# Two heads side by side in TensorE's rows, in scores and second GEMM, and another order of transposes between two batches

## The chip, the cores and the metric

The kernel runs on one core of one Trainium2 chip. The core has five engines with a queue each: TensorE (PE, matrix products into PSUM), VectorE (DVE), ScalarE (ACT), GpSimd (POOL) and SyncE (SP), which here only issues transfers (DMAs). An instruction starts when it has reached the head of its engine's queue and the semaphores that it waits for are set. The metric is the device time of one execution in microseconds (us).

## The reference

Eight batches of eight heads of causal attention over 576 tokens with 64 channels a head, with a forgetting factor that enters as a decay, then a dense layer pair with an exact GELU between:

```
scores = (q @ k^T) / 8 + (cum[s] - cum[t]), cum = cumsum(log(clip(f, 1e-4, 1)))
attn   = softmax(causal(scores));  x = attn @ v          # x as 4608 tokens x 512
out    = gelu(x @ w_in) @ w_out                          # 512 -> 2048 -> 512
```

Inputs and the output are float32; the kernel computes its products in bfloat16 with float32 sums.

## The kernel before

**Stages.** Each batch b has two stages. In its attention stage the four pairs of heads i = 0..3 go through scores, exp, and the product with v. In its first GEMM the 512 channels of x meet `w_in` in 16 blocks of 128 hidden channels, each four matmuls of 128x512, and GELU moves each block to SBUF as `g`. The second GEMM of batch b-1 is not a stage of its own: its 64 matmuls ("fill") are dealt out among the attention instructions of batch b by a table. 64 tokens of each batch (512 to 575, the "tail") don't fill a block of 128; they are collected in `tails` and go through both GEMMs at the end as a ninth block.

**Scores.** A pair's scores are held transposed, keys in partitions, in four PSUM tiles `s` with two banks each, one bank a head (tables `STILES`, with 448, 448, 448 and 320 columns a head). `kT[i]` holds the keys of both heads of pair i, one in partitions 0 to 63, one in 64 to 127. `qA[i]` and `qB[i]` hold one head's queries each in their half of the partitions and zeros in the other, so a matmul over all 128 partitions gives one head's scores (line 308). ACT takes exp of a whole tile (line 323), POOL sets what lies above the diagonal to zero (line 325); in batch 0 and the first pair of batch 1 PE adds a large negative number there instead (line 317). `s` tiles come from a pool of two, so scores of tile k wait until the exp of tile k-2 is done.

**Product with v.** `attend` (line 344) runs 15 small matmuls of 65 columns a head: v was multiplied by the decay weights on POOL (`weigh_v`, line 292), and its 65th column gives the softmax sum. `normalize` (lines 359 to 370) divides on DVE, into `x` and the tail `xt`. `x` has to be transposed for the first GEMM: SP issues a transposing DMA a pair (`x_dma`, line 386) and one for the tail (line 392). In batch 0 PE does it instead (`to_xT`, line 380).

**Queries and keys.** POOL's queue loads q and k of batch b+2 while batch b is worked on (line 102). Before the scores they are transposed: in batch 0 by PE (`transposes_first`), in batch 1 by PE (`transposes_pe`), from batch 2 on by transposing DMAs on SP (`transpose_dma`, line 262, four a batch: q and k, heads 0 to 3 and 4 to 7). DVE then sorts them into `qA`, `qB` and `kT` during the first GEMM of the batch before (`untangle`, line 276, eight copies a pair).

**What sets the order.** The program is scheduled by hand: each engine's instructions stand in the order in which the code emits them. `FILL[i][t]` says how many fill matmuls follow tile t of pair i, and its last row how many stand before, between and after the two heads of the last pair. `take(fill, n)` emits n of them; the generator `gemm2` opens a PSUM tile `ps` for every 128 tokens, sums over 16 blocks of hidden channels, and lets DVE copy the sum to SBUF (line 451) and SP store it (line 458).

Of the kernel before, what the change touches and what calls it, by code (L numbers as in the profile page):

```python
# [14 lines left out]
P = 128  # L15
# [35 lines left out]
def kernel(  # L51
# [96 lines left out]
    def zero_halves(pairs):  # L148
        for i in pairs:
            nc.vector.memset(qA[i][D:P, :], 0.0)  # L150
            nc.vector.memset(qB[i][0:D, :], 0.0)
# [23 lines left out]
    zero_halves(range(2))  # L175
# [16 lines left out]
    def transposes_first(i, which, pool, tag):  # L192

        src = qk_of[0][which]
        ps = pool.tile([P, JT, PT], BF16, tag=tag, name="ps_f")
        for h in range(2):
            for j in range(JT):
                nc.tensor.transpose(
                    ps[h * D : (h + 1) * D, j, :],
                    src[:, 2 * i + h, j * D : (j + 1) * D],  # L200
                    ident_bf[:PT, :PT],
                )

        def evac(eng, dst, r0, r1):
            op = eng.copy if eng is nc.scalar else eng.tensor_copy
            op(  # L206
                dst[r0:r1, :].rearrange("d (p j) -> d p j", j=JT),
                ps[r0:r1].rearrange("d j p -> d p j"),
            )

        if which:
            evac(nc.vector, kT[i], 0, P)
        else:
            evac(nc.vector if i else nc.scalar, qA[i], 0, D)
            evac(nc.vector, qB[i], D, P)

    def transposes_pe(b, i, pool):
# [20 lines left out]
        for which, ps in enumerate(pss):  # L238
            for h in range(2):
                dst = (qA[i], qB[i])[h] if which == 0 else kT[i]  # L240
# [26 lines left out]
    def untangle(b, i):  # L267

        for which, src in enumerate(tq_of[b]):
            for h in range(2):  # L270
                dst = (qA[i], qB[i])[h] if which == 0 else kT[i]
# [30 lines left out]
    def scores(b, i, t):  # L302
# [3 lines left out]
        for n, q0, w in STILES[t]:  # L306
            for h, qt in enumerate((qA[i], qB[i])):
                nc.tensor.matmul(  # L308
                    st[:, h, c : c + w],
                    kT[i][:, K0[n] : K0[n] + P],  # L310
                    qt[:, q0 : q0 + w],
# [65 lines left out]
    def to_xT(b, i, copy):  # L377
        ps = m_psum.tile([P, TC], BF16, tag="m", name="ps_x")
# [83 lines left out]

    def take(gen, n):
# [5 lines left out]
    def first_attention():  # L469
# [12 lines left out]
        zero_halves(range(2, HP))  # L482
# [55 lines left out]
    FILL = [[4, 6, 2, 2], [2, 2, 2, 2], [2, 2, 2, 2], [2, 2, 1, 1], [8, 0, 20]]  # L538
    FILL_1 = [[0, 4, 4, 0], [2, 2, 2, 2], [4, 4, 4, 4], [3, 3, 3, 3], [8, 0, 99]]

    def attention(b, fill, counts):
        for i in range(HP):
            for t in range(4):
# [6 lines left out]
                elif i and t == 3:  # L550
                    attend(b, i - 1, 1, (0, 1, 2, 3, 4))
                    normalize(b, i - 1, 1)
                    x_dma(b, i - 1)
                if t == 1 and i == 0 and b > 1:
                    load_v(b + 1)
                if b > 2 and t == 0 and i < 2:
                    transpose_dma(b + 1, 4 * i, 4 * i + 4)
                if b == 2 and t == 3 and i in (1, 2):
                    transpose_dma(3, 4 * i - 4, 4 * i)
                if b == 1 and (i, t) in ((0, 0), (0, 3)):  # L560
                    transposes_pe(1, 2 + t // 3, o_psum)
                if b == 1 and i == 1 and t in (0, 2):
                    weigh_v(1, 2 + t // 2)
                if b == 1 and i in (1, 2) and t == 3:
                    load_v(2, 4 * i - 4, 4 * i)
                take(fill, counts[i][t])
        i = HP - 1
        take(fill, counts[HP][0])
        attend(b, i, 0, (0, 1, 2, 3, 4))
# [4 lines left out]
        x_dma(b, i)  # L574
        x_tail_dma(b)
        if b == 1:
            transpose_dma(2, 0, 4)
            transpose_dma(2, 4, 8)
        take(fill, 999)

    for b in range(B):
        if b == 0:
            first_attention()
        else:
            attention(b, gemm2(b - 1, b == 1), FILL_1 if b == 1 else FILL)
# [3 lines left out]
        for ffb in range(n_ff):  # L589
            gemm1(b, ffb)  # L590
            if b == 0:
                if ffb in (6, 8):
                    transposes_pe(1, ffb // 2 - 3, s_psum)
# [47 lines left out]
```

## Time and profile before

| | us |
|---|---|
| median of 8 runs | 363.63 (362.56 to 364.57) |
| the profiled execution | 364.02 |
| its span, first to last instruction | 362.3 |
| PE busy in the span | 346.0 |
| ACT, DVE, POOL busy | 217.5, 179.4, 124.6 |
| time between the same points of two batches, 4 to 7 | 37.4 |

A row of the timeline gives start, length, engine, line and operation, output and inputs by name, shapes, the number of instructions that the row merges, and in square brackets how long the engine stood idle before it and what it waited for. Matmuls are pipelined: each is shown with its whole way through the array, so neighbours overlap, and the rate is read from the distance of two starts. A row of the table by stretches gives, for each engine, the busy time and in brackets the number of instructions, then the granted TensorE clock as a share of full speed, the busy share of the DMA engines, and GB/s.

### The profile page before, as it was taken

To read this page: it belongs to the slowest core of one execution; us is meant where nothing else is said; L and a number is where in the kernel's file an instruction comes from. 1 tells how busy PE (TensorE), PEld (TensorE's weight loads), DVE (VectorE), ACT (ScalarE), POOL (GpSimd) and SP (SyncE) were. 2 spreads that over 40 slices of the span, in tenths; PEclk is the share of its full clock that TensorE was granted. 3 is DMA by queue.
4 is the path that set the end of the run, shared out by engine and by line. 5 is a ranking of instruction groups with operands and counts; after the bars stand their busy time and mean duration, and the time that the engine had idled before them with its cause. 6 is when DMAs were issued, how large, how long until landed. Compare 5 with 4: busy or idle time off the path is not lost.

```text
span 362.3 us, 7046 instructions
## 1 busy us (share of the span) xinstructions
PE 346.0 (95%) x2740; PEld 188.6 (52%) x2740; DVE 179.4 (50%) x478; ACT 217.5 (60%) x298; POOL 124.6 (34%) x243
## 2 busy tenths in 40 slices
PE   7989989798998999999999999999999999999995
PEld 3764556433554456545654466446644664444443
DVE  7862884412966904592559446753676252011011
ACT  5887776255970788368845884578647973602610
POOL 7390284520447025621463055505440440000000
PEclk9999999989999999999999999999999999999999
DMA  7999999799758996397839792979520032011013
GB/s 111 169 189 191 181 171 212 173 123 198 136 125 137 191 191 123 77 179 146 160 77 168 146 188 63 150 130 207 87 81 0 34 71 80 2 58 58 2 29 87
DMA packets 106112, 44.38 MB, mean 122 GB/s; under 512 B 84896, under 2 KB 101536, under 8 KB 106080
## 3 DMA queue, kind: packets, MB, share of 16 engines
q1 hardware_dynamic: 88784, 29.78, 40.7%
q0 software_dynamic: 16896, 13.63, 25.8%
q8 instruction: 21, 0.34, 0.4%
q10 hardware_dynamic: 400, 0.52, 0.4%
q14 instruction: 11, 0.09, 0.1%
HBM read 36.85 MB, written 9.44 MB: 128 GB/s over the span
## 4 chain that ended last, share of the span: by engine, by line
PE 75%; DMA 10%; SPq 5%; DVE 4%; POOL 4%; issue 1%; POOLq 0%
PE ps L442 31%; PE ps L404 27%; PE s L308 10%; PE o L344 7%; DMA v_sb<-in_v_dram 4%; DMA tk<-k 4%; SPq L114 4%; DMA w_out_sb<-in_moe_w_out_dram 2%; DVE kT L276 1%; POOL vw L292 1%; DMA xT<-x 1%; POOL k L102 1%; DVE ot L451 1%; POOL q L102 1%; DVE qA L276 1%
## 5 line engine op out<-in xcount | busy, mean ns | idle before, releaser
L416 ACT ACTIVATE g<-ps 128x512 bf16<-128x512 f32 x144 | 86.0, 597 | 101.9 <-PE ps L404 101.8
L442 PE MATMUL ps<-w_out_sb,g 128*128 128x512 bf16 (+2 forms) x592 | 143.6, 373 | 1.3 <-DMA w_out_sb<-in_moe_w_out_dram 1.3
L404 PE MATMUL ps<-xT,w_in_sb 128*128 128x512 bf16 x512 | 115.0, 383 | 4.4 <-DMA xT<-x 3.7
L323 ACT ACTIVATE e<-s 128x896 bf16<-128x896 f32 (+1 forms) x128 | 105.3, 863 | 20.7 <-PE s L308 13.6
L325 POOL TENSOR_SCALAR_AFFINE_SELECT e<-e 128x256 bf16<-128x256 bf16 x135 | 54.2, 412 | 134.1 <-ACT e L323 132.9
L404 PEld LDWEIGHTS <-w_in_sb 128*128 128x128 bf16 x576 | 56.5, 98 | 74.9 <-issue 10.8
L451 DVE COPY ot<-ps 128x512 f32<-128x512 f32 (+2 forms) x37 | 25.1, 677 | 101.7 <-PE ps L442 101.5
L442 PEld LDWEIGHTS <-g 128*128 128x128 bf16 x592 | 52.2, 98 | 43.5 <-issue 1.5
L308 PE MATMUL s<-qA,kT 128*128 128x256 bf16 (+2 forms) x192 | 51.7, 281 | 2.6 <-DVE kT L276 1.5
L308 PEld LDWEIGHTS <-kT 128*128 128x128 bf16 x384 | 36.3, 97 | 33.8 <-issue 4.5
L292 POOL TENSOR_TENSOR vw<-v_sb,wT 128x640 bf16<-128x640 f32 x32 | 41.0, 1280 | 36.4 <-DMA v_sb<-in_v_dram 22.8
L308 PE MATMUL s<-qB,kT 128*128 128x256 bf16 (+2 forms) x192 | 48.3, 281 | 0.5 <-DVE qB L206 0.5
L344 PE MATMUL o<-vw,e 128*128 128x65 bf16 x960 | 43.1, 194 | 1.6 <-DVE xt L370 1.0
L344 PEld LDWEIGHTS <-e 128*128 128x128 bf16 x960 | 39.5, 98 | 9.1 <-issue 1.4
L276 DVE COPY kT<-tk 64x288 bf16<-64x288 bf16 x96 | 32.4, 338 | 8.6 <-DMA tk<-k 7.3
L359 DVE RECIPROCAL r<-o 128x5 f32<-128x5 f32 x64 | 12.4, 194 | 42.0 <-PE o L344 41.4
L360 DVE TENSOR_TENSOR x<-o,r 128x256 bf16<-128x256 f32 x64 | 27.2, 425 | 2.2
L276 DVE COPY qA<-tq 64x288 bf16<-64x288 bf16 x48 | 17.5, 366 | 10.0 <-DMA tq<-q 9.0
L370 DVE TENSOR_SCALAR xt<-o,r 64x64 bf16<-64x64 f32 x60 | 17.5, 291 | 1.4
L276 DVE COPY qB<-tq 64x288 bf16<-64x288 bf16 x48 | 17.1, 356 | 0.7
L404 PE MATMUL ps<-tails,w_in_sb 128*128 128x512 bf16 x64 | 14.3, 377 | 0.0
L416 ACT ACT_TABLE_LOAD x8 | 10.3, 1283 | 0.1
(63 smaller groups left out, 116.1 us busy)
## 6 DMA issues: line engine op xcount, KB each, us to landing
out_dram<-ot SPq DMA_DIRECT2D x32, 256.0 KB, 2.3
v_sb<-in_v_dram SPq DMA_DIRECT2D x20, 256.0 KB, 4.7
v_sb<-in_v_dram SPq DMA_DIRECT2D x29, 128.0 KB, 5.9
q<-in_q_dram POOLq DMA_DIRECT2D x6, 576.0 KB, 7.5
k<-in_k_dram POOLq DMA_DIRECT2D x6, 576.0 KB, 10.1
w_in_sb<-in_moe_w_in_dram POOLq DMA_DIRECT2D x4, 512.0 KB, 8.0
w_out_sb<-in_moe_w_out_dram POOLq DMA_DIRECT2D x4, 512.0 KB, 9.5
q<-in_q_dram POOLq DMA_DIRECT2D x4, 144.0 KB, 4.9
```

The costliest lines, as they stand in the source:

```text
L276: nc.vector.tensor_copy(rows[:, odd], src[odd * D : (odd + 1) * D, 2 * i + h].rearrange("d j p -> d p j"),)
L292: nc.gpsimd.tensor_tensor(vw_of[b][:, hs, :, 0:D], v_sb[:, hs, :, :], w.unsqueeze(3).to_broadcast([P, 2, NBLK, D]), Alu.mult,)
L308: nc.tensor.matmul(st[:, h, c : c + w], kT[i][:, K0[n] : K0[n] + P], qt[:, q0 : q0 + w], start=True, stop=not on_pe or c not in SDIAG[t],)
L323: nc.scalar.activation(et[:, :, 0:c], st[:, :, 0:c], Act.Exp, scale=scale)
L325: nc.gpsimd.affine_select(out=et[:, :, c0 : c0 + P], in_=et[:, :, c0 : c0 + P], compare_op=Alu.is_ge, fill=0.0, base=0, pattern=[[0, 2], [ ...
L344: nc.tensor.matmul(o[:, m, :], e_of[b, i, t][:, h, c : c + P], vw_of[b][:, 2 * i + h, n, :], start=(n == 0), stop=(n == m),)
L360: nc.vector.tensor_tensor(x_of[b, i][:, :, h, :], o[:, 0:4, 0:D], r[:, 0:4].unsqueeze(2).to_broadcast([P, NBLK - 1, D]), Alu.mult,)
L370: nc.vector.tensor_scalar(*tail, r[D:P, 4:5], None, Alu.mult)
L404: nc.tensor.matmul(ps, w_in_sb[:, kt, ffb * P : (ffb + 1) * P], src[:, kt, :], start=(kt == 0), stop=(kt == n_dm - 1),)
L416: nc.scalar.activation(g_of[c][ffb], ps, Act.Gelu)
L442: nc.tensor.matmul(pss[ts][:, c0:c1], g_of[c][kt][:, ts * P : (ts + 1) * P], w_out_sb[:, kt, c0:c1], start=(kt == 0), stop=(kt == n_ff - 1),)
L451: nc.vector.tensor_copy(ot[:, c0:c1], pss[ts][:, c0:c1])
```

## The change

Six edits, all of them in how the same results are made.

1. `qA` and `qB` become one tile `qT[i]` with the two heads' queries in its two halves of the partitions, and the zeroing of halves goes away. A score matmul takes 64 partitions of `kT` and `qT`: the first head's lie in rows 0 to 63 of the array, the second's in rows 64 to 127. In the first batch the queries go to SBUF in one copy a pair instead of two.
2. From batch 2 on the second GEMM that is dealt out among the scores is made by `gemm2_rows`. A step "r" is two matmuls of 64 rows, one from each half of the hidden block, into two PSUM banks; a step "n" is one matmul over all 128 rows into the first bank, as before. `STEPS` says which is which: "n" where the product with v is near, "r" elsewhere. DVE copies the second bank to SBUF and adds the first to it. Of 64 steps a batch 51 are "r".
3. The attention of those batches is in another order: both heads of pair i-1 stand together after the second score tile of pair i, and the table of fills differs.
4. The last pair's x of every batch from 1 on, and the last two of batches 1 and 2, are transposed by PE between fill matmuls, copied by DVE, with no DMA.
5. In batch 1, SP's order changes: the q, k of batch 2, heads 0 to 3, are transposed after the third pair, and the second half of v is loaded behind all four transposes. In batch 2 the four transposes for batch 3 stand together.
6. The third pair's q, k of batch 1 are transposed by PE within the first GEMM of batch 0 (after block 13), no longer in the attention of batch 1.

SP's queue at the end of batch 1, before (`tq`, `tk`: transposed q and k of batch 2; `v_sb`: v of batch 2):

```order
L114 DMA v_sb<-in_v_dram 128x4x64 x4
L114 DMA v_sb<-in_v_dram 64x4x64
L458 DMA out_dram<-ot 128x512
L386 DMA_TRANSPOSE xT<-x 128x4x128 x2
L392 DMA_TRANSPOSE tails<-xt 128x4x64
L262 DMA_TRANSPOSE tq_1242<-q_788 128x12x96
L262 DMA_TRANSPOSE tk_1243<-k_789 128x12x96
L262 DMA_TRANSPOSE tq_1242<-q_788 128x12x96
L262 DMA_TRANSPOSE tk_1243<-k_789 128x12x96
```

and with the change:

```order
L374 DMA_TRANSPOSE xT<-x 128x4x128
L249 DMA_TRANSPOSE tq_1078<-q_772 128x12x96
L249 DMA_TRANSPOSE tk_1079<-k_773 128x12x96
L446 DMA out_dram<-ot 128x512
L380 DMA_TRANSPOSE tails<-xt 128x4x64
L249 DMA_TRANSPOSE tq_1078<-q_772 128x12x96
L249 DMA_TRANSPOSE tk_1079<-k_773 128x12x96
L114 DMA v_sb<-in_v_dram 128x4x64 x4
L114 DMA v_sb<-in_v_dram 64x4x64
```

Two transposes of x are gone, the first two of q and k stand ahead of the tail's, and the second half of v stands last.

PE's queue in batch 2, the first score tile of the third pair and what stands around it, before (`g`: a hidden block after GELU; `ps`: sums of the second GEMM; `s`: scores):

```order
L442 MATMUL ps_1501<-w_out_sb,g_1276 128x512
L308 LDWEIGHTS kT_142
L308 MATMUL s_1561<-qA_134,kT_142 128x256
L308 LDWEIGHTS kT_142
L308 MATMUL s_1561<-qB_138,kT_142 128x256
L308 LDWEIGHTS kT_142
L308 MATMUL s_1561<-qA_134,kT_142 128x192
L308 LDWEIGHTS kT_142
L308 MATMUL s_1561<-qB_138,kT_142 128x192
L442 LDWEIGHTS g_1277
```

and with the change:

```order
L479 LDWEIGHTS g_1276
L479 MATMUL ps_1489<-w_out_sb,g_1276 128x512
L479 LDWEIGHTS g_1276
L479 MATMUL ps_1490<-w_out_sb,g_1276 128x512
L296 LDWEIGHTS kT_138
L296 MATMUL s_1593<-qT_134,kT_138 128x256
L296 LDWEIGHTS kT_138
L296 MATMUL s_1593<-qT_134,kT_138 128x256
L296 LDWEIGHTS kT_138
L296 MATMUL s_1593<-qT_134,kT_138 128x192
```

The score matmuls are as many as before, and each hidden block now has two matmuls, into the two banks `ps_1489` and `ps_1490`.

DVE's queue in batch 3, around the end of the second 128 tokens of the second GEMM, with the change (`L487` the copy of the second bank, `L489` the sum; before, a copy alone stood there):

```order
L358 TENSOR_SCALAR xt<-o,r 64x64
L487 COPY ot<-ps_2097 128x512
L489 TENSOR_TENSOR ot<-ot,ps_2096 128x512
L347 RECIPROCAL r<-o 128x5
L348 TENSOR_TENSOR x<-o,r 128x4x64
L358 TENSOR_SCALAR xt<-o,r 64x64
```

The sum stands ahead of the division of the second pair's first head.

The diff, cut to its core:

```diff
-    qA = [consts.tile([P, S], BF16, name=f"qA{i}") for i in range(HP)]
-    qB = [consts.tile([P, S], BF16, name=f"qB{i}") for i in range(HP)]
+    qT = [consts.tile([P, S], BF16, name=f"qT{i}") for i in range(HP)]
...
-            for h, qt in enumerate((qA[i], qB[i])):
+            for h in range(2):
+                d = slice(h * D, (h + 1) * D)
                 nc.tensor.matmul(
                     st[:, h, c : c + w],
-                    kT[i][:, K0[n] : K0[n] + P],
-                    qt[:, q0 : q0 + w],
+                    kT[i][d, K0[n] : K0[n] + P],
+                    qT[i][d, q0 : q0 + w],
...
+    STEPS = [
+        16 * "r",
+        5 * "r" + 2 * "n" + 8 * "r" + "n",
+        9 * "r" + 2 * "n" + 5 * "r",
+        8 * "r" + 8 * "n",
+    ]
+
+    def gemm2_rows(c):
+        for ts, steps in enumerate(STEPS):
+            if ts < n_sub - 1:
+                pool, tag = (m_psum, "m") if ts else (o_psum, "o")
+                banks = [
+                    pool.tile([P, d_model], FP32, tag=tag, name="ps2")
+                    for _ in range(2)
+                ]
+            else:
+                both = s_psum.tile([P, 2, d_model], FP32, tag="s", name="ps2")
+                banks = [both[:, 0], both[:, 1]]
+            ot = o_pool.tile([P, d_model], FP32, tag="ot", name="ot")
+            for kt, step in enumerate(steps):
+                last = kt == steps.rindex("r")
+                for r in range(2 if step == "r" else 1):
+                    rows = slice(r * D, (r + 1) * D) if step == "r" else slice(0, P)
+                    nc.tensor.matmul(
+                        banks[r],
+                        g_of[c][kt][rows, ts * P : (ts + 1) * P],
+                        w_out_sb[rows, kt, :],
+                        start=(kt == 0),
+                        stop=last if r else kt == n_ff - 1,
+                    )
+                if kt == n_ff - 1 if ts == n_sub - 1 else last:
+                    nc.vector.tensor_copy(ot, banks[1])
+                if kt == n_ff - 1:
+                    nc.vector.tensor_tensor(ot, ot, banks[0], Alu.add)
...
-    FILL = [[4, 6, 2, 2], [2, 2, 2, 2], [2, 2, 2, 2], [2, 2, 1, 1], [8, 0, 20]]
+    FILL = [[6, 5, 4, 3], [0, 3, 3, 2], [0, 3, 3, 3], [0, 3, 3, 2], [8]]
+    FILL_AV = [2, 1, 2, 2]
...
+    def attention(b):
+        fill = gemm2_rows(b - 1)
+
+        def av(i):
+            for h in range(2):
+                attend(b, i, h, (0, 1, 2, 3, 4))
+                if h == 0:
+                    take(fill, FILL_AV[i])
+                normalize(b, i, h)
+
+        for i in range(HP):
+            for t in range(4):
+                scores(b, i, t)
+                take(fill, FILL[i][t])
+                if i and t == 1:
+                    av(i - 1)
+                    if i < HP - 1 or b > 2:
+                        x_dma(b, i - 1)
...
+        take(fill, FILL[HP][0])
+        if b == 2:
+            to_xT(b, HP - 2, nc.vector.tensor_copy, o_psum, "o")
+        av(HP - 1)
+        take(fill, 5)
+        to_xT(b, HP - 1, nc.vector.tensor_copy, o_psum, "o")
+        x_tail_dma(b)
+        take(fill, 999)
...
+    def second_attention():
+        b, fill, counts = 1, gemm2(0, True), FILL_1
...
+                if t == 3:
+                    if i == 1:
+                        load_v(2, 0, 4)
+                    if i == 2:
+                        transpose_dma(2, 0, 4)
                 take(fill, counts[i][t])
...
+        to_xT(b, i, nc.vector.tensor_copy, o_psum, "o")
         x_tail_dma(b)
-        if b == 1:
-            transpose_dma(2, 0, 4)
-            transpose_dma(2, 4, 8)
+        transpose_dma(2, 4, 8)
+        load_v(2, 4, 8)
         take(fill, 999)
```

More of the change, by code (lines that the diff above doesn't have):

```diff
@@ L174 @@
     nc.vector.memset(ones, 1.0)
-    zero_halves(range(2))
     nc.vector.memset(wT[0:D, 4, :], 0.0)
@@ L202, in transposes_first @@
                 )
[L204 to L215, printed above, removed]
+        op = nc.scalar.copy if i == 0 and not which else nc.vector.tensor_copy
+        op(
+            (qT, kT)[which][i].rearrange("d (p j) -> d p j", j=JT),
+            ps.rearrange("d j p -> d p j"),
+        )
     def transposes_pe(b, i, pool):
```

58 lines of the change are left out of this document (31 added, 27 removed).

## The prediction

> **What bounds the kernel now.** I read the page first, then the busy time by stretches, cut at the borders of the stages.
>
> ```profile
> PE 346.0 (95%) x2740; PEld 188.6 (52%) x2740; DVE 179.4 (50%) x478; ACT 217.5 (60%) x298; POOL 124.6 (34%) x243
> ```
>
> ```profile
> 69.60:89.40 19.80, 16.01 (x65) 6.59 (x63) 3.29 (x9) 9.55 (x16) 4.81 (x8) 0.91 1.05 155
> 89.40:114.00 24.60, 23.56 (x233) 14.37 (x234) 18.30 (x51) 15.65 (x18) 12.39 (x26) 1.00 0.77 146
> 114.00:129.50 15.50, 14.07 (x65) 6.22 (x64) 11.87 (x33) 8.96 (x15) 3.20 (x5) 1.00 0.99 161
> ...
> 153.20:167.00 13.80, 13.80 (x66) 6.21 (x64) 11.86 (x33) 8.96 (x15) 3.09 (x5) 1.00 0.81 145
> 167.00:190.60 23.60, 23.60 (x234) 14.32 (x233) 9.36 (x27) 16.22 (x19) 12.11 (x26) 1.00 0.68 137
> ```
>
> The last two rows are a steady batch: first GEMM 13.80 us, attention stage 23.60 us, PE busy throughout. The first three are the same stages of batches 1 and 2 (first GEMM, attention, first GEMM): 19.80 + 24.60 + 15.50 = 59.90 us, against 13.80 + 23.60 + 13.80 = 51.20 in the steady state. So two things can be had: PE's own work in the steady stages, and 8.7 us lost between 69.6 and 129.5. What ends the gaps there, on PE's timeline:
>
> ```profile
> 71.91 0.38 PE L404 MATMUL ps<-xT,w_in_sb 128*128 128x512 bf16 x1 [1.69 <-DMA xT<-x]
> 72.91 15.01 PE L404 MATMUL ps<-xT,w_in_sb 128*128 128x512 bf16 x61 [0.62 <-DMA xT<-x]
> ...
> 89.44 0.28 PE L308 MATMUL s<-qA,kT 128*128 128x256 bf16 x1 [1.52 <-DVE kT L276]
> ...
> 100.43 0.35 PE L344 MATMUL o<-vw,e 128*128 128x65 bf16 x6 [1.00 <-DVE xt L370]
> ...
> 115.96 0.38 PE L404 MATMUL ps<-xT,w_in_sb 128*128 128x512 bf16 x1 [1.39 <-DMA xT<-x]
> ```
>
> Transposes of x come late twice, and the first pair of batch 2 waits for sorted keys. After the gaps the clock is down (0.91 in its stretch): the x61 row takes 15.01 us, where 61/64 of 13.80 is 13.2. Why the keys are late:
>
> ```profile
> 65.49 2.85 SPq L114 DMA_DIRECT2D v_sb<-in_v_dram  x5
> ...
> 69.08 2.55 SPq L386 DMA_TRANSPOSE xT<-x  x2
> ...
> 73.01 1.33 SPq L262 DMA_TRANSPOSE tq<-q  x1
> 74.43 1.93 SPq L262 DMA_TRANSPOSE tk<-k  x1
> 76.41 6.19 SPq L262 DMA_TRANSPOSE tq<-q  x1
> 82.66 5.13 SPq L262 DMA_TRANSPOSE tk<-k  x1
> ...
> 79.44 0.67 DVE L276 COPY qA<-tq 64x288 bf16<-64x288 bf16 x2 [9.00 <-DMA tq<-q]
> ...
> 88.05 1.33 DVE L276 COPY kT<-tk 64x288 bf16<-64x288 bf16 x4 [7.26 <-DMA tk<-k]
> ...
> 73.50 0.82 POOL L102 DMA_DIRECT2D q<-in_q_dram  x1
> ```
>
> The first keys were issued at 74.43 and arrive at 88.05, because POOL starts loading batch 3's q and k at 73.50 on the same DMA engines. DVE then sorts late into batch 2's attention, which is the 1.00 at 100.43.
>
> **The change, part by part.**
>
> *Edits 4 and 5, batches 1 and 2.* The first GEMM of batch 1 no longer waits for a transposing DMA of its last two pairs; 8 PE transposes and two DVE copies stand among fill. The transposes of q and k, heads 0 to 3, are issued after the third pair, where the later half of v stood (65.49), so 7.5 us ahead of 73.01. That half of v now comes behind all four; POOL weighs it before it loads batch 3's q and k, so that load starts later than 73.50 and no longer meets the transposes. The 1.69, 0.62, 1.52, the slow clock (15.01 - 13.2 = 1.8) and the 1.00 go. What becomes late next: batch 3's q and k land later, and the four transposes of batch 3, which stand together on SP in batch 2, wait for them; behind these stands the second x transpose of batch 2, which the first GEMM of batch 2 needs. By the rows above, what the DMA engines had to move from 73.50 on took until 88, 14 us; with a start at 81 to 83 (tail, two transposes, v and its weighing follow each other from 70 on) they land at about 96, the four issues (1.3 to 1.9 us each) end at 102, and the x lands some 4 us on, about when that GEMM starts (107). I keep 0.5 us for that. The gap of 1.39 and what comes with it goes too. Of 8.7 us I take 8.2; bounds 3 (the x of batch 2 late by several us, with a slow clock after it) and 8.7.
>
> *Edit 1, scores.* Rates, from the same batch:
>
> ```profile
> 173.47 0.35 PE L308 MATMUL s<-qA,kT 128*128 128x448 bf16 x1
> 173.65 0.35 PE L308 MATMUL s<-qB,kT 128*128 128x448 bf16 x1
> 173.84 0.45 PE L344 MATMUL o<-vw,e 128*128 128x65 bf16 x9
> ...
> 174.83 0.64 PE L344 MATMUL o<-vw,e 128*128 128x65 bf16 x15
> 175.31 0.59 PE L442 MATMUL ps<-w_out_sb,g 128*128 128x512 bf16 x2
> ```
>
> Start to start, 448 columns take 0.19 us. A pair has 1664 columns a head, so 2 x 1664/448 x 0.19 = 1.40 us, a batch 5.6. If the two heads run at once, half of that goes: 2.8 us a batch. Fifteen small matmuls take 0.48 us; that an LDWEIGHTS and a matmul pass in 0.032 us each time shows that doubling the instructions of a fill step (13.80/64 = 0.216 us) fills no queue.
>
> Do the halves of the array run at once, and what does it cost to go from one division to another? No matmul pair of the new kind is in this trace. The nearest rows are batch 0's transposes `ps_f`, which use 64 columns of the array at a time, and `psw` with 64 rows:
>
> ```profile
> 9.09 0.21 PE L198 MATMUL ps_f<-ident_bf,q 96*64 96x96 bf16 x1
> 9.12 0.21 PE L198 MATMUL ps_f<-ident_bf,k 96*64 96x96 bf16 x1
> 9.13 0.21 PE L198 MATMUL ps_f<-ident_bf,q 96*64 96x96 bf16 x1
> 9.16 0.21 PE L198 MATMUL ps_f<-ident_bf,k 96*64 96x96 bf16 x1
> ...
> 16.17 0.28 PE L317 MATMUL s<-after,ident_bf 128*128 128x128 bf16 x2
> 16.28 0.25 PE L308 MATMUL s<-qA,kT 128*128 128x192 bf16 x1
> ...
> 9.95 0.28 PE L317 MATMUL s<-after,ident_bf 128*128 128x128 bf16 x2
> 10.16 0.27 PE L489 MATMUL psw<-ident_fp,f_sb 64*128 64x64 f32 x1
> ```
>
> q and k, in different halves, alternate, and each stream keeps 0.04 us for its 96 columns, which is 96/448 of 0.19: two streams, no loss. Bounds for a pair of 512 columns: 0.216 (both at once) and 0.431 (one after the other). I take 0.216, since the only two streams that the trace has lose nothing. Two 128-column matmuls are followed after 0.11 us when the division stays, after 0.21 when it changes: a change costs 0.10 us.
>
> *Edits 2 and 3, the steady attention stage.* Going through the new order with these durations: the division changes 8 times a batch (in at the first score tile; out and in around three products with v; out before the fourth): +0.8. Four PE transposes for the last x: +0.2. The r steps cost nothing by the price taken. New waits: with the scores shorter, PE reaches the score tile that waits for exp sooner.
>
> ```profile
> 169.06 6.73 ACT L323 ACTIVATE e<-s 128x896 bf16<-128x896 f32 x8
> 176.40 3.48 ACT L323 ACTIVATE e<-s 128x896 bf16<-128x896 f32 x4 [0.61 <-PE s L308]
> ...
> 176.04 0.25 PE L308 MATMUL s<-qB,kT 128*128 128x192 bf16 x1
> ```
>
> And from the table of groups by form, with busy time and mean ns of one behind the bar:
>
> ```profile
> L323 ACT ACTIVATE e<-s 128x640 bf16<-128x640 f32 x32 | 22.5, 704 | 2.4 <-PE s L308 0.8 <-PE s L317 0.6
> L451 DVE COPY ot<-ps 128x512 f32<-128x512 f32 x35 | 24.2, 692 | 99.5 <-PE ps L442 99.2
> L360 DVE TENSOR_TENSOR x<-o,r 128x256 bf16<-128x256 f32 x64 | 27.2, 425 | 2.2
> ```
>
> The exp starts 0.11 after the end of its scores (176.04 + 0.25 to 176.40). A pair's fourth tile, in halves, takes 0.14 us on PE; its exp starts 0.41 after the tile begins, runs 0.70, and frees its buffer at 1.15. PE meanwhile does 0.14, two fills (0.43) and the next pair's first tile (0.19), and stands at the second tile at 0.76: it waits 0.4, or 0.2 where three fills stand between. Over three pairs 0.8. The third tile of the batch waits for the first exp, which a table load holds back to about 2.1 us after the stage begins: 0.2. In the third block of 128 tokens the bank is free only when DVE has added the second block's sums: 0.3 from the matmul's end to DVE's start, then a sum of 512 columns, about 0.7 (the copy 0.69; the 256-column operation 0.43 and 256 more columns), together 1.0, of which 0.76 lie behind the other head's product (0.48), a change (0.10) and a score tile (0.19): 0.3. Sum of waits 1.3; 0.3 of that kind stand in the stage now. The rest is covered: the four sums on DVE (2.8 us) by its idle time (9.36 busy of 23.60), the last x's copy (about 1 us behind its transposes) by the last fill and the first three matmuls of the GEMM. Per batch: -2.8 + 0.8 + 0.2 + 1.0 = -0.8; I take -0.7, for the second stream starts about 0.03 us behind the first at each change (0.1). Six batches (2 to 7): **-4.2**. Bounds: -1.7 each if the waits don't come (-10), and no gain if a pair costs 0.23 instead of 0.216 (51 x 0.014 = 0.7).
>
> *Batches 0 and 1.* There each mask on PE and each fill (still over 128 rows) stands between scores: in batch 0 some 40 changes (+4.0) against 2.8 saved; edit 6 puts 12 transposes of 0.04 (0.5) ahead. All of this is ahead of a wait that stays:
>
> ```profile
> 49.80 0.38 PE L442 MATMUL ps<-w_out_sb,g 128*128 128x512 bf16 x1 [1.31 <-DMA w_out_sb<-in_moe_w_out_dram]
> ```
>
> The 1.31 covers +1.7 in part, and the rest is covered as the order now puts a score tile, part of a product and no transposes (0.5) ahead of this matmul. If that cover were gone, it would cost up to 1 us. After it 20 more changes (+2.0) stand against 1.9 saved and 0.2 of transposes added: **+0.3**.
>
> Sum: -8.2 - 4.2 + 0.3 = -12.1. The profiled execution took 364.02 us (span 362.3, 1.7 outside it); the median of the runs is 0.4 lower, so 363.63 - 12.1 = **351.5**.
>
> **The rivals.**
> *A, the steady stages gain nothing:* exp, DVE's sum and the changes take all of 2.8. For it: by the sum only 0.8 of 2.8 is left. Against: the waits were taken at their full length. Time 363.6 - 8.2 + 0.3 = 355.7.
> *B, the stall moves to batch 2:* batch 3's q and k come so late that SP stands, the x of batch 2 is late by 3 to 4 us and the clock drops. For it: the 14 us of landing above, in which a load held other transfers back. Against: two of four x are no longer in that queue. Time about 351.5 + 5 = 356.5.
> *C, slower: two row halves don't run at full rate,* since both add into PSUM over all 128 partitions, where the column halves of `ps_f` each wrote only their own 64. The place is the 51 r steps of six batches, 306 pairs. The gain is gone from 12.1/306 = 0.040 us a pair on, that is a pitch above 0.256. A third of the way from 0.216 to 0.431, 0.288, gives +22: 373.6. Against: the rows of `ps_f`.
> The Trainium skill ("TensorE: Matmul & The Clock Gate", "Measured speedup vs the span model") gives 3.07 times for four row tiles, 77% of what four streams could do; a pair would then take an estimated 0.28 us and the kernel 371. The same page's span model (4 ns for each further tile) speaks for 351.5. By the first, rival C holds; the trace's two streams agree with the second. No run here shows row tiles yet.
> *D, better:* the waits on exp and on the bank don't come, -1.0 a batch: 345.5.
>
> **How the numbers follow.** Forecast 0.50, A 0.17, B 0.14, C 0.13, D 0.06. What a measurement of this kernel can tell from no change is 0.3%, 1.1 us. C alone ends at or above 362.5, and a mild C (0.25 us a pair) is within that bound: faster 0.85, same 0.03, slower 0.12. The range reaches from D to a C that takes nearly all: 345 to 362; the forecast's own is 348 to 355.
>
> **What would show it.** Pairs of 512 columns at 0.216 us from pair to pair in PE's timeline (0.25 or more: C). 0.10 us at each change of division. A steady attention stage of 22.7 to 23.0 us and still 13.8 for the first GEMM; waits of PE on exp of 0.2 to 0.4 at three places, on DVE's sum once. In batch 1's first GEMM no wait for `xT` and the clock at 1.00; the first score of batch 2 at 84, of batch 3 at about 121. A wait on `xT` in batch 2's first GEMM of over 1 us would show B.

## The result and the profile after

The changed kernel takes 353.23 us (median of 11 runs, 351.81 to 357.31), the kernel before, on the same chips, 363.55 (31 runs, 360.72 to 364.57). The ratio of the means is 0.9726, with a 95% interval of 0.9702 to 0.9749: faster by 2.7%; the slowest of the 11 runs, in which the granted clock was lower, is left out of the ratio. The forecast was 351.5, in a range of 345 to 362. The profiled execution took 353.65 us, 351.6 of it span and 2.0 outside.

The page's engine line of the changed kernel, and its clock in 40 slices:

```profile
PE 338.9 (96%) x3082; PEld 174.7 (50%) x3082; DVE 203.0 (58%) x499; ACT 216.2 (61%) x298; POOL 124.5 (35%) x243
PEclk9999999999999999999999999999999999999999
```

PE is still the bound. It has 342 instructions more and is busy 7.1 us less; DVE is busy 23.6 us more.

The busy time of the changed kernel by stretches, cut at its own stages: the first GEMM of batch 1, attention and first GEMM of batch 2, and a first GEMM and an attention stage of the steady batches:

```profile
72.20:86.10 13.90, 13.90 (x66) 6.16 (x66) 13.38 (x33) 8.96 (x15) 4.75 (x7) 1.00 0.58 136
86.10:109.00 22.90, 22.60 (x293) 13.07 (x293) 11.99 (x33) 16.06 (x19) 9.25 (x23) 1.00 1.12 186
109.00:123.20 14.20, 14.08 (x67) 6.15 (x67) 13.68 (x33) 8.96 (x15) 6.07 (x10) 1.00 0.70 127
...
145.80:159.70 13.90, 13.90 (x65) 6.16 (x63) 13.39 (x32) 8.96 (x15) 6.12 (x10) 1.00 0.68 108
159.70:182.40 22.70, 22.40 (x289) 12.85 (x289) 12.58 (x35) 16.06 (x19) 9.16 (x22) 1.00 0.91 158
```

The three stages that took 59.90 us take 51.0, about what they take in the steady state, and the clock stays at 1.00. In the first GEMM of batch 1 nothing waits any more: PE's timeline shows it as one row of 64 matmuls, where before two waits for `xT` cut it up.

```profile
72.18 13.97 PE L392 MATMUL ps<-xT,w_in_sb 128*128 128x512 bf16 x64
```

SP's queue and DVE around it show why the keys are now in time (`tq`, `tk`: transposed q and k of batch 2):

```profile
64.80 2.02 SPq L374 DMA_TRANSPOSE xT<-x  x1
66.91 1.30 SPq L249 DMA_TRANSPOSE tq<-q  x1
68.31 1.71 SPq L249 DMA_TRANSPOSE tk<-k  x1
...
72.91 1.34 DVE L263 COPY qT<-tq 64x288 bf16<-64x288 bf16 x4
...
84.55 1.75 DVE L263 COPY kT<-tk 64x288 bf16<-64x288 bf16 x4
...
84.52 0.82 POOL L102 DMA_DIRECT2D q<-in_q_dram  x1
```

The first queries are issued at 66.91 instead of 73.01, DVE sorts from 72.91 instead of 79.44, and POOL's load of batch 3's q and k starts at 84.52 instead of 73.50, when only the last 4 of the 32 sorting copies (84.55) are still to come.

The difference by stretches of the two profiled executions, against the prediction's terms. The borders are the starts of PE's first score and first GEMM matmul of each batch:

| stretch | before, us | after, us | difference | predicted |
|---|---|---|---|---|
| up to the first GEMM of batch 1 | 69.63 | 72.18 | +2.55 | +0.3 |
| from there to the scores of batch 3 | 59.90 | 50.98 | -8.92 | -8.2 - 0.7 |
| batches 3 to 7, five times 37.42 and 36.57 | 187.1 | 182.8 | -4.3 | -3.5 |
| outside the span | 1.7 | 2.0 | +0.3 | 0 |

The rest, the tail's two GEMMs at the end, is the same within 0.03. So the two gains came about as forecast, and between these two executions one term, the smallest, came at more than eight times its size.

### The profile page after: what moved, and what is told of

Same layout as the page of the kernel before. It is cut to its first block, busy times and chain, and to the rows that moved or that the text cites. A ratio compares the mean times of both kernels' runs of the same rounds, so it can differ in the third digit from the quotient of the medians.

```text
span 351.6 us, 7729 instructions
## 1 busy us (share of the span) xinstructions
PE 338.9 (96%) x3082; PEld 174.7 (50%) x3082; DVE 203.0 (58%) x499; ACT 216.2 (61%) x298; POOL 124.5 (35%) x243
## 4 chain that ended last, share of the span: by engine, by line
PE 75%; ACT 7%; DMA 7%; SPq 4%; POOL 4%; issue 1%; DVE 0%; POOLq 0%; ACTq 0%; DVEq 0%
PE ps L392 32%; PE ps L479 18%; PE ps L430 11%; PE o L332 8%; PE s L296 6%; DMA v_sb<-in_v_dram 4%; SPq L114 4%; ACT e L311 4%; ACT L311 2%; DMA w_out_sb<-in_moe_w_out_dram 2%; POOL vw L279 1%; ACT g L404 1%; POOL k L102 1%; DMA xT<-x 1%; POOL q L102 1%
## 5 line engine op out<-in xcount | busy, mean ns | idle before, releaser
L479 PE MATMUL ps<-w_out_sb,g 64*128 64x512 bf16 (+1 forms) x690 | 102.3, 376 | 0.0
L296 PE MATMUL s<-qT,kT 64*128 64x320 bf16 (+4 forms) x384 | 47.8, 282 | 4.0 <-ACT e L311 3.4
L479 PEld LDWEIGHTS <-g 64*128 64x128 bf16 (+1 forms) x690 | 37.6, 94 | 25.5 <-issue 1.6
L263 DVE COPY qT<-tq 64x288 bf16<-64x288 bf16 x96 | 45.1, 470 | 1.5
L430 PE MATMUL ps<-w_out_sb,g 128*128 128x512 bf16 (+2 forms) x208 | 44.3, 363 | 0.9 <-DMA w_out_sb<-in_moe_w_out_dram 0.9
L487 DVE COPY ot<-ps 128x512 f32<-128x512 f32 x24 | 16.5, 688 | 36.2 <-PE ps L479 36.2
L439 DVE COPY ot<-ps 128x512 f32<-128x512 f32 (+2 forms) x13 | 8.4, 649 | 48.9 <-PE ps L430 48.7
L296 PEld LDWEIGHTS <-kT 64*128 64x128 bf16 x384 | 20.0, 93 | 28.7 <-issue 15.6
L430 PEld LDWEIGHTS <-g 128*128 128x128 bf16 x208 | 18.8, 97 | 20.0 <-issue 1.4
L489 DVE TENSOR_TENSOR ot<-ot,ps 128x512 f32<-128x512 f32 x24 | 16.5, 687 | 1.3
```

Of the source, the lines that this page charges most:

```text
L263: nc.vector.tensor_copy(rows[:, odd], src[odd * D : (odd + 1) * D, 2 * i + h].rearrange("d j p -> d p j"),)
L296: nc.tensor.matmul(st[:, h, c : c + w], kT[i][d, K0[n] : K0[n] + P], qT[i][d, q0 : q0 + w], start=True, stop=not on_pe or c not in SDIAG[t],)
L430: nc.tensor.matmul(pss[ts][:, c0:c1], g_of[c][kt][:, ts * P : (ts + 1) * P], w_out_sb[:, kt, c0:c1], start=(kt == 0), stop=(kt == n_ff - 1),)
L479: nc.tensor.matmul(banks[r], g_of[c][kt][rows, ts * P : (ts + 1) * P], w_out_sb[rows, kt, :], start=(kt == 0), stop=last if r else kt == n ...
```

## The experiments

Each was timed on chips that ran the kernel before as well: 363.77 (first four), 363.78 (next four) and 364.07 us (last two). "From the first GEMM of batch 1" is what one profiled execution took from that point to its end. What lies ahead of that point differs from run to run by more than most of the effects (last section), so the columns are read apart. The ratios are of means, so they differ a little from the quotients of the medians.

| kernel | median, us | ratio to before, 95% | first GEMM of batch 1 starts | from there to the end |
|---|---|---|---|---|
| before | 363.55 | | 69.63 | 292.7 |
| the change | 353.23 | 0.9726 (0.9702 to 0.9749) | 72.18 | 279.4 |
| e1_order | 357.86 | 0.9832 (0.9773 to 0.9892) | 71.49 | 284.9 |
| e2_rows | 365.41 | 1.0044 (1.0021 to 1.0068) | 70.29 | 293.9 |
| e3_full_fill | 358.37 | 0.9841 (0.9791 to 0.9891) | 70.72 | 285.7 |
| e4_no_rows | 357.91 | 0.9833 (0.9783 to 0.9884) | 69.87 | 284.8 |
| e5_fill | 349.60 | 0.9654 (0.9592 to 0.9715) | 70.66 | 276.6 |
| e6_third_back | 352.49 | 0.9702 (0.9679 to 0.9726) | 72.44 | 279.7 |
| e9_no_pe_x | 360.19 | 0.9901 (0.9868 to 0.9934) | 71.70 | 285.0 |
| e10_old_queue | 356.25 | 0.9785 (0.9740 to 0.9830) | 70.36 | 281.1 |
| e11_fill_split | 348.66 | 0.9583 (0.9556 to 0.9610) | 70.91 | 275.4 |
| e12_w_out | 349.11 | 0.9624 (0.9579 to 0.9669) | 71.66 | 275.4 |

### The two halves of the change apart

**Edits 4, 5 and 6 alone**, on the kernel before: in batches 1 and 2 PE transposes the same x as in the change (from batch 3 on the last x still goes by DMA), SP's order and the third pair are as in the change, but scores and fill go over all 128 rows, from batch 2 on in the old order.

```diff
-                    x_dma(b, i - 1)
+                    if i < HP - 1 or b > 2:
+                        x_dma(b, i - 1)
...
+                    if i == 1:
+                        load_v(2, 0, 4)
+                    if i == 2:
+                        transpose_dma(2, 0, 4)
...
+        to_xT(b, i - 1, nc.vector.tensor_copy, o_psum, "o")
```

> The kernel before with the edits at the border of batches 1 and 2 alone (x of the last pairs transposed by PE, the queue order of SyncE, the third pair's q, k in the first GEMM); no division of the array. Theory (the two sources add up): the lost 8.7 us of batches 1 and 2 come back and nothing else, 354.5 to 356.0 us; batch 1's first GEMM 13.8 to 13.9 us, a steady batch 37.4 us as before. Rival (the stalls went because the shorter scores moved the work, and come back without it): 358 us or more, with waits on xT or on sorted keys in batches 1 and 2.

Measured 357.86, between the two theories. The profile decides for the first: from the first GEMM of batch 1 to the scores of batch 3 it has stages of 13.81, 24.24 and 13.89 us, 8.0 less than before, and no wait for `xT` or keys. What is missing lies ahead of that. In the profiled execution its first score starts at 8.74 instead of 7.43, with the same code ahead of it, and 0.5 is edit 6, which makes the first GEMM of batch 0 longer (15.54 instead of 15.02). The third score tile of batch 1:

```profile
47.48 0.35 PE L308 MATMUL s<-qA,kT 128*128 128x448 bf16 x1 [0.98 <-ACT e L323]
```

In the kernel before this tile waited 0.47 for exp (at 45.69). The transposes that stood between the two tiles ahead of it are now in the first GEMM, and the tile waits the longer: edit 6 moves 0.5 us of work, and batch 1's attention gets no shorter by it (27.12 against 27.05).

**Edits 1, 2 and 3**, with edit 6: the change with edits 4 and 5 undone in batches 1 and 2. From batch 3 on PE still transposes the last x.

```diff
-                    if i < HP - 1:
-                        x_dma(b, i - 1)
+                    x_dma(b, i - 1)
...
-        to_xT(b, i, nc.vector.tensor_copy, o_psum, "o")
+        x_dma(b, i)
         x_tail_dma(b)
+        transpose_dma(2, 0, 4)
```

> The changed kernel without the edits at the border of batches 1 and 2: all four x of batches 1 and 2 go by transposing DMA again, SyncE's queue has the order of before there; heads and halves side by side stay. Theory (additive): 353.2 + 8 = 361 us (360 to 362), steady batches 36.6 us, the waits on xT and on keys of batches 1 and 2 back. Rival (the queue order hardly matters, the rows bring nearly all): 355 us or less.

Measured 365.41, 0.4% above the kernel before, where both theories had it below. Adding up the terms fails here: the steady stages have their gain (22.67 and 13.91), but the attention of batch 2 takes 29.02 where the kernel before took 24.53, and the first GEMM of batch 2 17.92 where it took 15.56. PE's timeline of this kernel has the old waits for `xT`, the last of them longer than before (2.16 against 1.39), and one wait that the kernel before didn't have, on `ot`:

```profile
72.78 0.38 PE L392 MATMUL ps<-xT,w_in_sb 128*128 128x512 bf16 x1 [1.90 <-DMA xT<-x]
...
99.44 0.99 PE L332 MATMUL o<-vw,e 128*128 128x65 bf16 x15 [4.01 <-DVE ot L487]
...
120.75 15.01 PE L392 MATMUL ps<-xT,w_in_sb 128*128 128x512 bf16 x60 [2.16 <-DMA xT<-x]
```

DVE's timeline of the same kernel just ahead of the wait on `ot`:

```profile
95.52 1.80 DVE L263 COPY qT<-tq 64x288 bf16<-64x288 bf16 x4
97.33 1.34 DVE L263 COPY kT<-tk 64x288 bf16<-64x288 bf16 x4
98.70 0.69 DVE L487 COPY ot<-ps 128x512 f32<-128x512 f32 x1
99.42 0.69 DVE L489 TENSOR_TENSOR ot<-ot,ps 128x512 f32<-128x512 f32 x1
```

The first block of `gemm2_rows` holds both banks of the pool from which the product with v takes its own. They come free by DVE's copy and sum, and these stand in DVE's queue behind the sorting of q and k, which ends at 98.67 because the keys are late. So the row-divided second GEMM makes DVE's queue a link in PE's chain, and needs keys that are early. The prediction had the two parts as independent terms.

**Edit 4 undone alone**, in batches 1 and 2 (e9_no_pe_x), and **edit 5 undone alone** (e10_old_queue, with the four transposes of batch 2 parted again too), in this order:

```diff
-        to_xT(b, i - 1, nc.vector.tensor_copy, o_psum, "o")
...
-        to_xT(b, i, nc.vector.tensor_copy, o_psum, "o")
+        x_dma(b, i)
```

```diff
-                    if i == 1:
-                        load_v(2, 0, 4)
-                    if i == 2:
-                        transpose_dma(2, 0, 4)
+                    load_v(2, 4 * i - 4, 4 * i)
...
+        transpose_dma(2, 0, 4)
```

> The changed kernel with all x of batches 1 and 2 by transposing DMA; SyncE's order of q, k and v stays as in the change. Theory (x of the last pairs late, keys early): waits on xT of about 2.2 us and a slow clock of 1.8 in batch 1's first GEMM, about 1.5 in batch 2's, no wait for keys: 357 to 359 us. Rival (only the queue order mattered): 353 to 354 us.

> The changed kernel with SyncE's order of v, q and k in batches 1 and 2 as before; the last x of batches 1 and 2 still by PE. Theory (keys late: VectorE sorts them into batch 2's attention, and the first sums of the second GEMM, which hold both banks of the product with v, stand behind that sorting): batch 1's first GEMM 13.9 us, but batch 2's attention 25 to 28 us, 356 to 359 us. Rival (with two transposes less in the queue the keys come early enough): 353 to 354 us.

Without edit 4 the time is 360.19, 7.0 more than the change and above the 357 to 359 expected, and batch 1's first GEMM waits for `xT` twice and then runs at a lower clock, as before the change:

```profile
74.07 0.38 PE L392 MATMUL ps<-xT,w_in_sb 128*128 128x512 bf16 x1 [1.78 <-DMA xT<-x]
75.35 14.85 PE L392 MATMUL ps<-xT,w_in_sb 128*128 128x512 bf16 x61 [0.90 <-DMA xT<-x]
...
71.70:90.10 18.40, 15.72 (x65) 6.51 (x63) 12.07 (x33) 8.96 (x15) 4.93 (x8) 0.91 0.66 150
```

Without edit 5 it is 356.25, 3.0 more, as its theory had it; x is in time, half of the keys come late, and the link that e2_rows showed is there in a smaller size:

```profile
92.41 0.63 PE L332 MATMUL o<-vw,e 128*128 128x65 bf16 x15 [1.93 <-DVE ot L487]
```

The transposes of heads 0 to 3, issued at 70.22 and 71.61, are sorted from 73.66 and 75.41 on; for those of heads 4 to 7, issued at 73.19 and 75.06, DVE waits until 84.61 and 86.77. So the late ones are those under way beside POOL's load of batch 3's q and k (73.26), as the prediction had it.

Undone alone the two edits cost 7.0 and 3.0, undone together 12.2, more than their sum. From the first GEMM of batch 1 on it is 5.6, 1.7 and 14.4 in the profiled executions; but those of e9_no_pe_x and e10_old_queue were the fastest of their four (358.41 and 353.34), so the gap between 14.4 and the sum is too large there, and the medians are the fairer measure.

### What the row halves are worth

**The change with no division of the rows:** its order, its table of fills and its transposes, but zero-padded queries and a second GEMM over 128 rows into one bank.

```diff
-            for h in range(2):
-                d = slice(h * D, (h + 1) * D)
+            for h, qt in enumerate((qA[i], qB[i])):
...
-                    kT[i][d, K0[n] : K0[n] + P],
-                    qT[i][d, q0 : q0 + w],
+                    kT[i][:, K0[n] : K0[n] + P],
+                    qt[:, q0 : q0 + w],
...
-                        g_of[c][kt][rows, ts * P : (ts + 1) * P],
+                    g_of[c][kt][:, ts * P : (ts + 1) * P],
```

> The changed kernel with no division of the array by rows at all: scores with zero halves over 128 rows as before, the second GEMM over 128 rows; order, fills and queues of the change stay. Theory (rows save 2.8 us of scores a batch and cost 0.8 in changes and about 1 in waits): +0.9 to +1.2 a batch over six batches, less the 1 to 2 us that the changes of division cost in batches 0 and 1: 357 to 360 us; an attention stage of 23.5 to 23.9 us. Rival (the new order of fills and products brings the steady gain, the rows nothing): 353 us.

**The change with row halves in the scores alone:** the fill as in e4_no_rows, so that the division (all 128 rows, or two halves of 64) changes at every fill.

> The changed kernel with the second GEMM of batches 1 to 6 over all 128 rows and into one bank (no steps r, no sums on VectorE); scores stay divided, the tables of fills stay. Theory (0.10 us at each change of division, on the path): 26 changes a batch instead of 8, +1.8 us, less 0.2 for the bank's wait: +1.6 x 6 = +9.6, about 363 us; an attention stage of 24.2 us. Rival (the changes hide in the 1.3 us of waits for exp that stand there anyway): +0.5 a batch, 356 to 357 us.

A steady attention stage of e4_no_rows, then of e3_full_fill:

```profile
158.90:182.60 23.70, 23.42 (x232) 14.49 (x236) 10.29 (x31) 16.50 (x19) 9.17 (x21) 1.00 0.80 151
```

```profile
161.00:184.50 23.50, 22.84 (x232) 11.58 (x237) 10.21 (x30) 16.46 (x19) 9.16 (x21) 1.00 0.79 152
```

Measured 357.91 and 358.37: the first as its theory had it, the second between its theory (363) and its rival (356 to 357), nearer to the rival. Without division the stage is 23.70, against 23.60 in the kernel before: the new order by itself gains nothing. Halves in the scores alone bring it to 23.50, so 2.8 us of PE time saved in scores are nearly all given back. With the fill divided too it is 22.70. That is rival A's mechanism, and it shows what edit 2 is for: the fill itself is no faster in halves, but it keeps the division where it is. PE's timeline of e3_full_fill has the change at each fill:

```profile
160.99 0.37 PE L296 MATMUL s<-qT,kT 64*128 64x256 bf16 x4
161.29 1.47 PE L473 MATMUL ps<-w_out_sb,g 128*128 128x512 bf16 x6
162.69 0.37 PE L296 MATMUL s<-qT,kT 64*128 64x320 bf16 x4
162.99 0.82 PE L473 MATMUL ps<-w_out_sb,g 128*128 128x512 bf16 x3
```

From the scores to the fill it takes 0.30 here, 0.20 in the change (123.16 to 123.36, below). The 18 more changes of a batch would be 1.8; the stage lost 0.8 to 0.9. As the matmuls are the same work, the rest must have gone into waits that are there in any case, for exp and for DVE's sum; no row shows which. This kernel also has rival B's wait, 1.10 for `xT` in the first GEMM of batch 2.

### Two versions that beat the change

**Another table of fills:** one fill step moved ahead of the second tile of each pair, where PE waited for exp.

```diff
-    FILL = [[6, 5, 4, 3], [0, 3, 3, 2], [0, 3, 3, 3], [0, 3, 3, 2], [8]]
+    FILL = [[6, 6, 3, 3], [1, 2, 3, 2], [1, 2, 3, 3], [1, 2, 3, 2], [8]]
```

> The changed kernel with fill steps moved within each pair of batches 2 to 7, from before a product with v to between the two score tiles that stand side by side (0,3 becomes 1,2), and one step earlier in the first pair; all counts at the products stay. Theory (PE's remaining waits for exp stand at the second tile of each pair and the third of the batch, about 1.1 us a batch, and a fill step of 0.216 us there replaces that much of each): -0.75 us a batch, six batches -4.5: 348.7 us, attention stage 21.9 us. Rival (exp itself is the bound of the stage, so the wait only moves to the next tile): 353 us, the stage 22.6 us.

Measured 349.60; the interval of its ratio just overlaps that of the change. The steady attention stage:

```profile
157.90:179.90 22.00, 21.98 (x288) 12.79 (x288) 12.52 (x34) 16.00 (x19) 9.13 (x21) 1.00 0.89 164
```

The stage is 0.7 shorter with the same work: most of the waits were schedule, not a limit, and the stage of rival D (22.7 to 23.0 less 1.0) is to be had. But with batch 2 shorter, rival B's mechanism comes up. PE in the first GEMM of batch 2, and SP's queue ahead of it:

```profile
108.25 13.76 PE L392 MATMUL ps<-xT,w_in_sb 128*128 128x512 bf16 x63 [1.05 <-DMA xT<-x]
...
100.69 2.74 SPq L249 DMA_TRANSPOSE tq<-q  x1
103.48 1.35 SPq L249 DMA_TRANSPOSE tk<-k  x1
105.80 1.22 SPq L374 DMA_TRANSPOSE xT<-x  x1
```

The x transpose stands behind the transposes of batch 3's q and k and is issued at 105.80, 2.4 us ahead of the matmul that needs it.

**The four transposes parted again**, heads 0 to 3 ahead of that x and heads 4 to 7 behind it, as in the kernel before:

```diff
-                if b == 2 and t == 1 and i == 1:
-                    transpose_dma(3, 0, 4)
-                    transpose_dma(3, 4, 8)
+                if b == 2 and t == 1 and i in (1, 2):
+                    transpose_dma(3, 4 * i - 4, 4 * i)
```

> The kernel with moved fills (349.6 us) and, in batch 2, SyncE's four transposes for batch 3 parted again: heads 0 to 3 after the first x transpose, heads 4 to 7 after the second. Theory (in batch 2 the second x transpose stands behind all four, is issued at 105.8 and lands 1.05 us too late for the first GEMM): it is issued some 4 us sooner, the wait on xT is gone, batch 2's first GEMM takes 13.9 instead of 15.1 us, 348.5 us. Rival (the DMA engines, not the queue's order, make it late): 349.6 us, the wait stays.

Measured 348.66, the lowest median of all (4.2% below the kernel before). By the intervals it can't be told from e5_fill, but the profile shows the step: the x is issued 4.1 us earlier, the wait is gone and batch 2's first GEMM takes 13.91 instead of 15.12.

```profile
101.72 1.88 SPq L374 DMA_TRANSPOSE xT<-x  x1
```

### The start

**Edit 6 undone:** the third pair of batch 1 transposed within its attention, as before.

```diff
-                if (i, t) == (0, 2):
-                    transposes_pe(1, 3, o_psum)
+                if (i, t) in ((0, 0), (0, 3)):
+                    transposes_pe(1, 2 + t // 3, o_psum)
...
-                if ffb in (6, 8, 13):
+                if ffb in (6, 8):
```

> The changed kernel with the third pair's q, k of batch 1 transposed in batch 1's attention again, as before. Theory (batch 1's first score tiles wait for exp, 0.96 and 0.55 us, so PE has that room for 0.5 us of transposes, and moving them ahead only lengthened the first GEMM by 0.5): first GEMM of batch 0 15.1 us instead of 15.6, batch 1's attention as long as before, 352.7 us. Rival (the move ahead takes 0.5 us out of batch 1's attention, VectorE's copies included): 353.7 us or more.

Measured 352.49 against 353.23, with overlapping intervals: inconclusive. The wait for exp at batch 1's third tile is 0.45 here, 0.96 in the change, which agrees with e1_order, but a new wait of 1.18 for POOL's mask follows, and in its profiled execution the first GEMM of batch 0 ran at a granted clock of 0.90 (16.62 us).

**`w_out` earlier:** e11_fill_split with the second quarter of `w_out` ahead of the first weighing of batch 1 on POOL.

```diff
+            load_w_out(1)
...
-                    for c in range(1, 4):
+                    for c in range(2, 4):
```

> The kernel of the run beside it and GpSimd's queue with the second quarter of w_out loaded before, not after, the weighing of batch 1's first v. Theory (PE's wait for w_out in batch 1, 0.9 us in the changed kernel's profile, is set by the transfers, which are all busy then, not by the queue: the quarter comes earlier, but batch 1's v comes later by what it takes): the wait moves from w_out to the weighed v, 348 to 349.5 us, no gain beyond 0.5. Rival (the queue's order sets it): the wait is gone and nothing takes its place, 1 us or more faster than the run beside it.

Measured 349.11 against 348.66, no gain, as the theory had it. POOL's first weighing of batch 1 starts at 45.80 instead of 43.05, so v did come later; but the wait for `w_out` that was to be exchanged for it stands in neither profile. It stands in 3 of the 12 profiles, those of the kernel before, the change and e9_no_pe_x.

## Why the prediction was right, and where it was not

**Edits 4 and 5: right.** -8.9 with batch 2's share of the rows, as forecast. All waits named are gone. The first scores of batches 2 and 3 start at 86.09 and 123.16, not at 84 and about 121, because the start before them took 2.55 more. The next thing late is where the prediction put it: the first GEMM of batch 2 has 0.3 more than a steady one (14.19 against 13.91), for the `xT` that SP issued at 107.01, where 0.5 was kept. Rival B was near: 1.10 and 1.05 in two kernels of other timing.

**Edit 1 and rival C: right.** The rows of PE's timeline of the changed kernel, at the start of batch 3's attention:

```profile
123.16 0.36 PE L296 MATMUL s<-qT,kT 64*128 64x256 bf16 x4
123.36 1.46 PE L479 MATMUL ps<-w_out_sb,g 64*128 64x512 bf16 x12
124.66 0.35 PE L296 MATMUL s<-qT,kT 64*128 64x320 bf16 x4
124.85 1.24 PE L479 MATMUL ps<-w_out_sb,g 64*128 64x512 bf16 x10
126.14 0.36 PE L296 MATMUL s<-qT,kT 64*128 64x448 bf16 x2
...
127.97 0.75 PE L296 MATMUL s<-qT,kT 64*128 64x256 bf16 x8
128.55 0.82 PE L479 MATMUL ps<-w_out_sb,g 64*128 64x512 bf16 x6
129.31 0.65 PE L332 MATMUL o<-vw,e 128*128 128x65 bf16 x15
129.79 0.59 PE L479 MATMUL ps<-w_out_sb,g 128*128 128x512 bf16 x2
130.22 0.64 PE L332 MATMUL o<-vw,e 128*128 128x65 bf16 x15
130.79 0.36 PE L296 MATMUL s<-qT,kT 64*128 64x448 bf16 x2
...
132.22 0.37 PE L296 MATMUL s<-qT,kT 64*128 64x256 bf16 x4
132.82 0.37 PE L296 MATMUL s<-qT,kT 64*128 64x320 bf16 x4 [0.23 <-ACT e L311]
133.01 0.83 PE L479 MATMUL ps<-w_out_sb,g 64*128 64x512 bf16 x6
```

Six pairs of row halves take 1.30 us (123.36 to 124.66), 0.216 each. A tile's 448 columns of both heads take 0.20 where they took 0.38. Rival C needed 0.256.

The Trainium skill ("TensorE: Matmul & The Clock Gate", "Measured speedup vs the span model") gives 3.07 times for four row tiles, from which the prediction worked out an estimated 0.28 us a pair. For two row tiles in a steady stream the trace has 0.216, which agrees with the span model in the same section of the Trainium skill; no run here has four row tiles, so the 3.07 itself is not tried.

**Edits 2 and 3: right.** A change of division: three pairs from 128.55 end at 129.20, the product starts at 129.31, so 0.11; the product's 0.48 from 130.22 ends at 130.70, the scores start at 130.79, so 0.09. Forecast 0.10. The waits: the five pairs from 124.85 end at 125.93 and the third tile starts at 126.14, 0.21; two tiles from 127.97 take 0.58 where 0.38 is their rate, 0.20; from 132.22 to 133.01 it is 0.79 where 0.38 is, 0.41. These were forecast as 0.2, 0.2 and 0.4, and the second tile of the last pair, forecast at 0.2, starts 0.17 late at 137.20. The wait for DVE's sum, forecast at 0.3, came as 0.17 and for one row half alone (last section). A steady stage came out at 22.7, the lower end of 22.7 to 23.0, and a batch at -0.85 instead of -0.7.

**Batches 0 and 1: wrong.** The step that failed is "All of this is ahead of a wait that stays", which made +0.3 of the work added there. The wait for `w_out` is not a fixed point. The row in the changed kernel, with the two waits for exp ahead of it:

```profile
46.90 0.36 PE L296 MATMUL s<-qT,kT 64*128 64x448 bf16 x2 [0.96 <-ACT e L311]
...
50.17 0.37 PE L296 MATMUL s<-qT,kT 64*128 64x320 bf16 x4 [0.55 <-ACT e L311]
...
51.77 0.59 PE L430 MATMUL ps<-w_out_sb,g 128*128 128x512 bf16 x2 [0.94 <-DMA w_out_sb<-in_moe_w_out_dram]
```

Here the transfer landed 2 us later than in the profile of before, where PE went on at 49.80. PE was there at 50.83, 1.0 after that point, and waited another 0.9. In the three profiles with this wait it ends 7.2 to 7.3 us after POOL's first weighing of batch 1 starts (at 42.61 before, 44.49 in the change, 44.73 in e9_no_pe_x), for the load of that part of `w_out` stands behind the weighing in POOL's queue, and the weighing waits for v. So the point moves with the landing of v.

In e2_rows, e3_full_fill, e5_fill, e10_old_queue and e11_fill_split, with the same code up to here, there was no wait for `w_out` at all. From the first score to the first GEMM of batch 1 those five need 62.8 to 63.4 us, before 62.2 with its wait of 1.31, the change 64.65. So the added work used up the cover of 1.31 and took 0.6 to 1.2 more, where +0.3 was forecast; the other 1.4 to 2.0 of this execution has 0.94 of wait in it. How much of that other executions of the change have isn't shown: the profiled one (353.65) is only 0.4 above their median. Of the 0.6 to 1.2, edit 6 has 0.5 in the first GEMM of batch 0. What the division of the scores costs there stays open: e1_order and e4_no_rows have edit 6 without it and need 62.75 and 62.40, and that is no further from the five than these are from each other.

**The terms as a sum: wrong in a way that the change didn't show.** With both halves of the change the terms add up to -12.1, against a measured -10.3. With one alone they don't add up: edits 1, 2, 3 and 6 without 4 and 5 cost 1.6 us (e2_rows), and given the other edits the row halves are worth 4.7 (e4_no_rows to the change).

## What to carry to other kernels

Two row halves side by side were worth having here where work of the same division stood next to them: divide the neighbours too, or the changes can eat the gain. Count the second bank's copy and sum as a link from the vector engine's queue to the matrix engine, and ask what may stand ahead of them in that queue. Don't lean a term of a sum on one transfer's landing in one execution of a start-up that is full of transfers: take added work ahead of it at its full price, or read that landing in several profiles.

## What the runs showed of the hardware that was not expected

Matmuls of different row halves don't keep the program's order. The changed kernel's PE and DVE timelines, where both heads' scores stand ahead of the next step of fill in the program:

```profile
134.67 0.69 DVE L489 TENSOR_TENSOR ot<-ot,ps 128x512 f32<-128x512 f32 x1
...
135.24 0.98 PE L479 MATMUL ps<-w_out_sb,g 64*128 64x512 bf16 x6
135.88 0.30 PE L296 MATMUL s<-qT,kT 64*128 64x320 bf16 x1
136.02 0.38 PE L479 MATMUL ps<-w_out_sb,g 64*128 64x512 bf16 x1
136.06 0.29 PE L296 MATMUL s<-qT,kT 64*128 64x320 bf16 x1
```

One half goes on to its fill at 136.02 while the other half's score, earlier in the program, starts at 136.06: each half keeps its own order, and one runs 0.17 us behind the other. The lag comes from DVE's sum, which ends at 135.36: within the row at 135.24 one half starts its fill at once, and the other, whose bank the sum reads, at 135.41. The same stands in the next four batches.

In the start the transfers land up to 2 us apart from one profile to another. POOL's first weighing of batch 1, which waits for v (in the profiles of e2_rows and e3_full_fill the releaser shown is PE), starts at 42.4 to 44.5 us in the profiles of the kernel before, the change and the first four experiments, with the same loads ahead of it in POOL's queue, and e1_order's first score 1.3 us after that of the kernel before. These are single executions of different kernels; how far one kernel's own executions differ there was not traced.
